# The first attention layer's opening, in a new order: single-ring loads, one row tile first, mask rows built between other steps

## The chip, the core and the metric

One core of a Trainium2 chip runs the whole program. The metric is device time in microseconds (us), from the median of several executions. One further execution was taken with the hardware profiler, and all durations below come from it. The engines are TensorE (PE, matmul), VectorE (DVE), ScalarE (ACT), GpSimd (POOL) and SyncE (SP, which only issues transfers). ACT and POOL can issue transfers too.

## The reference

Four layers, A B A B, over x of 2048 rows by 576, each with a layer norm in front and a residual behind. The change lies in the first A.

```python
def _A_ref(x, wqkv, wo):            # S = 2048, D = 576, H = 32 heads of Dh = 18
    W, dil = (8, 2)
    q, k, v = split(x @ wqkv)
    idx = pos[:, None] - arange(W) * dil      # each row looks at 8 rows, 2 apart
    mask = idx >= 0
    logits = where(mask, einsum(q, k[idx]) * Dh ** -0.5, -1e9)
    return einsum(softmax(logits), v[idx]) @ wo
x = x + _A_ref(_layernorm(x), A_wqkv, A_wo)
x = x + _B_ref(_layernorm(x), ...)           # gated MLP with a 2048 x 2048 row mix
x = x + _A_ref(_layernorm(x), A_wqkv, A_wo)
x = x + _B_ref(_layernorm(x), ...)
```

## The kernel before

x is cut into 16 row tiles of 128 rows. Each is normalised to bf16 (`ln_xn`, four buffers in rotation) and transposed into `xnT`, five chunks of 128 columns by all 2048 rows, from which everything else is projected.

Attention works on 19 query tiles (`NT`) of up to 112 rows, each with 16 rows of halo, in two half-steps of 16 heads, and takes dense 128 x 112 logits. Which keys a query may see is not masked afterwards. It is built into the product: Q and K of each head (18 rows) are extended to 32 rows in the tile `QK`, and the 14 added rows hold a fixed pattern whose product is strongly negative outside the window. The pattern repeats every 256 columns. `build_window_rows` (L115) makes one period in `win_rows`, stores it to DRAM (`win_period`, L166), `load_pat` (L168) reads it back four times into `win_pat`, and `fill_window_rows` (L181) copies it with DVE over one half of `QK`'s columns at a time (four copies of 4096 elements per partition, L190). Heads are then written over rows 0 to 17 of each group of 32.

The steps of the first layer's opening (L499 to L611), each a small function:

- `x_load`: a load of one to four row tiles. `load_wv`, `load_wqk`: the weights, 2 and 6 transfers.
- `S_`, `E_` on DVE: mean and variance of a tile (two L532 and one L533), plus epsilon (L536). `R_` on POOL: the power -1/2 (L539). `A_` on DVE: the normalised tile (L547).
- `T_pe`: five transposes on PE and a copy by ACT (L551, L556). `T_`: a transposing transfer on SP instead (L242).
- `VW(t, hh)` (L364): half of the values of query tile t, five matmuls, evacuated by ACT or DVE into `v_ext`. VW(t) needs rows 112t - 16 to 112t + 112. The last column of each head in `v_ext` holds ones (L517).
- `PG(d, qk, cc)` (L375): Q or K, columns 128d to 128d + 127, rows 512cc to 512cc + 511; five matmuls, evacuated into a staging tile `stg`. For the first 1024 rows, blocks d = 3 and 4 are staged in the space of `win2a` instead. When all parts of a block d for 1024 rows are there, it issues the head moves: one transfer of 72 KB per whole head from staging into `QK`, eight per block, dealt to the queues of POOL and SP in turn. For d = 4 the block holds Q and K side by side and only `PG(4, 0, cc)` exists.
- `L_mm(s)`, `EXP(s)`, `PV(s)` (L417, L431, L438): logits, exponential and value product of a half-step. `L_mm(0)` needs heads 0 to 15, `L_mm(1)` heads 16 to 31.

Behind the opening, the loop runs L_mm(s + 1), EXP(s + 1), PV(s) and whatever a table assigns to s: the remaining PGs (cc = 3 needs row tiles 12 to 15), values, the output projection, the next layer norm. Six PGs with cc = 2 stand between `L_mm(0)` and `L_mm(1)`.

What sets the order: `manual_schedule` (L341) keeps every engine's instructions in program order, so the order of the calls is the order on each engine and each queue. A transfer's issue blocks the issuing queue until its semaphores allow it. Transfers of SP and ACT share eight completion semaphores in rotation, so the issue also waits for the earlier transfer on the same semaphore.

The order before, around the PGs:

```python
order = [(d, cc) for cc in (0, 1) for d in (0, 1, 2)] + [(d, cc) for d in (3, 4) for cc in (0, 1)]
...
                if k_ == 3:
                    R_(8, 4)
                    A_(8, 9, 10, 11)
                    T_(8, 9, 10, 11)
                    S_(12, 13, 14, 15)
                    E_(12, 4)
                if k_ == 5:
                    self.fill_window_rows(QK, 1)
                    R_(12, 4)
                    A_(12, 13, 14, 15)
            T_(12, 13, 14, 15)
```

Of the kernel before, what the change touches and what calls it, by code (L numbers as in the profile page):

```python
# [10 lines left out]
ALU = mybir.AluOpType  # L11
AX = mybir.AxisListType
f32 = mybir.dt.float32
bf16 = mybir.dt.bfloat16
# [4 lines left out]
P = 128  # L19
D = 576  # L20
# [6 lines left out]
PADL = HALO  # L27
# [35 lines left out]
class K:  # L63
# [51 lines left out]
    def build_window_rows(self, c, eng):  # L115
# [31 lines left out]
        nc.vector.tensor_scalar(out=n[:], in0=n[:], scalar1=15, scalar2=None, op0=ALU.bitwise_and)  # L147
        nc.vector.tensor_scalar(out=g[:], in0=n[:], scalar1=1, scalar2=None, op0=ALU.logical_shift_right)
        nc.vector.tensor_tensor(out=g[:], in0=g[:], in1=n[:], op=ALU.bitwise_xor)
        for i in range(4):  # L150
            nc.vector.tensor_scalar(out=bits[:, i, :], in0=g[:], scalar1=i, scalar2=1,
                                    op0=ALU.logical_shift_right, op1=ALU.bitwise_and)
        nc.vector.tensor_scalar(out=bits[:, 4, :], in0=n[:], scalar1=1, scalar2=None, op0=ALU.bitwise_and)
        nc.vector.tensor_scalar(out=vf[:], in0=bits[:], scalar1=-2.0, scalar2=1.0, op0=ALU.mult, op1=ALU.add)
        nc.vector.tensor_scalar_mul(out=R[:, :, 0:8, :], in0=R[:, :, 0:8, :], scalar1=vf[:, 4, 1:2])
        nc.vector.tensor_tensor(out=uu[:], in0=vf[:, 0:4, 0:2], in1=vf[:, 0:4, 1:3], op=ALU.add)
        nc.vector.tensor_scalar_mul(out=R[:, 0, 8:12, :], in0=vf[:, 0:4, 1:2].to_broadcast([P, 4, 16]), scalar1=half)
        nc.vector.tensor_scalar_mul(out=R[:, 1, 8:12, 0:2], in0=uu[:, :, 0:1].to_broadcast([P, 4, 2]), scalar1=0.5)
        nc.vector.tensor_scalar_mul(out=R[:, 1, 8:12, 2:16], in0=uu[:, :, 1:2].to_broadcast([P, 4, 14]), scalar1=0.5)
        one = self.dram.tile([2, MR, 256], bf16, name="win_period")  # L160
        nc.gpsimd.memset(self.pat[:], 0.0)
        nc.gpsimd.memset(self.patpad[:], 0.0)
        for j in range(4):
            nc.gpsimd.affine_select(out=self.patpad[:], in_=self.patpad[:], compare_op=ALU.not_equal, fill=1.0,
                                    base=-32 * j - 31, pattern=[[0, PADL]], channel_multiplier=1)
        self.dma(one[:].rearrange("a r (p f) -> p (a r) f", f=16), R[0:16].rearrange("p a r f -> p (a r) f"), eng=eng)  # L166
# [4 lines left out]
        self.load_pat = load  # L171

    def make_ident(self):
        nc = self.nc
        for xb in self.xn_bufs:
            nc.gpsimd.memset(xb[:, D:640], 0.0)
        nc.gpsimd.memset(self.ident[:], 0.0)
        nc.gpsimd.affine_select(out=self.ident[:], in_=self.ident[:], compare_op=ALU.not_equal, fill=1.0,
                                base=0, pattern=[[-1, P]], channel_multiplier=1)
# [133 lines left out]
    def layer_A(self, li):  # L313
# [183 lines left out]


        if li == 0:  # L499
# [9 lines left out]
            x_load(x0[:, 0:2, :], 0, 2, nc.sync)  # L509
            x_load(x0[:, 2:4, :], 2, 2, nc.sync)  # L510
            self.load_wv(nc.scalar)
            x_load(x1[:, 0:4, :], 4, 4, nc.sync)
            self.load_wqk(nc.sync)
            self.zero_right()
            exp_table()
            self.build_window_rows(sb, nc.scalar)
            nc.scalar.copy(out=v_ext[:, :, :, DH:DH + 1], in_=self.ones[:, None, None, :].to_broadcast([P, NT, H, 1]))  # L517
            self.make_ident()
            setup_bufs(nc.gpsimd)
            x_load(spare, 8, 4, nc.sync)  # L520
            self.load_pat(nc.sync)
            warm = self.PT_tile([P, 512], f32, "warm")
            for _ in range(28):
                nc.tensor.matmul(warm[:, 0:P], lhsT=self.ident[:], rhs=self.ident[:], start=True, stop=True)
# [36 lines left out]
            S_(0, 1)  # L561
            E_(0, 2)
            R_(0, 2)
            S_(2)
            A_(0, 1)
            T_pe(0)
            T_pe(1)
            VW(0, 0, False)
            VW(0, 1, False)
            S_(3)  # L570
            E_(2, 2)
            R_(2, 2)
            VW(1, 0, False)
            VW(1, 1, False)
            S_(4)
# [3 lines left out]
            S_(5)  # L579
# [9 lines left out]
            R_(6, 2)  # L589
            A_(6, 7)  # L590
            T_(6, 7)
            x_load(sb.tile([P, 4, D], bf16, name="x_in3", tag="x_in", bufs=2)[:], 12, 4, nc.sync)
            self.fill_window_rows(QK, 0)
            S_(8, 9, 10, 11)
            E_(8, 4)
            order = [(d, cc) for cc in (0, 1) for d in (0, 1, 2)] + [(d, cc) for d in (3, 4) for cc in (0, 1)]
            for k_, (d, cc) in enumerate(order):
                for qk in ((1, 0) if d < 4 else (0,)):
                    PG(d, qk, cc, False, (nc.gpsimd, nc.sync) if d in (0, 4) else (nc.gpsimd, nc.gpsimd, nc.sync))
                if k_ == 3:  # L600
                    R_(8, 4)
                    A_(8, 9, 10, 11)
                    T_(8, 9, 10, 11)
                    S_(12, 13, 14, 15)
                    E_(12, 4)
                if k_ == 5:
                    self.fill_window_rows(QK, 1)
                    R_(12, 4)
                    A_(12, 13, 14, 15)
            T_(12, 13, 14, 15)  # L610
            nvw0, nvw = 3, 8  # L611
# [14 lines left out]
        q2 = (nc.gpsimd, nc.sync, nc.gpsimd)  # L626
# [395 lines left out]
```

The softmax here doesn't subtract the row's maximum and nothing guards it: scores larger than these inputs give would overflow.

## Time and profile before

| | us |
|---|---|
| median of 4 runs | 1202.51 (1200.61 to 1203.09) |
| the profiled execution, its own time | 1204.71 |
| its span, first to last instruction | 1202.9 |
| PE busy in the span | 1175.9 (98%) |
| DVE, ACT, POOL busy | 545.4, 377.9, 274.4 |
| first warm-up matmul; first VW; first PG | 5.71; 12.22; 18.48 |
| end of the last opening PG (d = 4, cc = 1) | 38.06 |

In the profile's rows, a line is: start, duration, engine, line of the code, operation, written tile <- read tiles, shape, count, and in brackets the engine's idle time before it and what ended that. SPq, ACTq are issues of transfers by those queues. A row of waits is: who <- for whom: us in total, times, longest. A row of windows is: the stretch, its length, then busy time and number of instructions of PE, PE's weight loads, DVE, ACT and POOL, then the granted PE clock (1.00 is full), the share of the transfer engines in use, and GB/s. A wait for several semaphores is put down to the one that the profile saw last.

### The profile page before, as it was taken

What the parts mean: (1) busy time and instruction counts of PE and PEld (TensorE: products, weight loads), DVE (VectorE), ACT (ScalarE), POOL (GpSimd) and SP (SyncE); (2) the same over time, 40 slices, a digit from 0 to 9 for tenths busy, and PEclk for the clock granted to TensorE, in tenths of its full rate; (3) what the DMA queues carried; (4) which work ended last, traced back from release to release, by engine and by line L of the source; (5) the groups of instructions that cost most, each with busy time, mean ns of one, the idle gap of its engine ahead of it and who ended that gap; (6) DMA issues with size and microseconds to landing.
All of it is one profiled execution on the core that took longest, in us unless ns stands there. A gap on an engine that the chain in (4) does not pass through costs nothing.

```text
span 1202.9 us, 20636 instructions
## 1 busy us (share of the span) xinstructions
PE 1175.9 (98%) x8438; PEld 620.6 (52%) x8536; DVE 545.4 (45%) x1199; ACT 377.9 (31%) x599; POOL 274.4 (23%) x381
## 2 busy tenths in 40 slices
PE   7899999999999999999999999999999999999998
PEld 4456644444444444447755765444444444444677
DVE  7577776432332332335454776763233323222321
ACT  4477777401111101101146786770110110111000
POOL 3558874100000000001135677640000000000000
PEclk9999999999999999999999999999999999999999
DMA  6789897000000000049646998900000000000432
GB/s 172 143 172 220 187 165 154 22 1 12 11 11 12 1 11 11 1 136 266 179 91 123 181 230 197 235 1 22 12 5 7 11 11 11 11 1 19 131 105 72
DMA packets 178185, 101.21 MB, mean 84 GB/s; under 512 B 135003, under 2 KB 159435, under 8 KB 178090
## 3 DMA queue, kind: packets, MB, share of 16 engines
q1 hardware_dynamic: 164330, 77.64, 30.6%
q0 software_dynamic: 6480, 15.96, 5.3%
q10 hardware_dynamic: 7280, 6.28, 1.7%
q8 instruction: 67, 1.10, 0.4%
q14 instruction: 28, 0.23, 0.1%
HBM read 42.39 MB, written 16.53 MB: 49 GB/s over the span
## 4 chain that ended last, share of the span: by engine, by line
PE 94%; DMA 3%; issue 1%; ACT 1%; POOL 1%; DVE 0%; SPq 0%; ACTq 0%; POOLq 0%; DVEq 0%
PE pg L856 41%; PE pz L838 12%; PE po L910 12%; PE pz L760 11%; PE pp L391 4%; PE pv L368 4%; PE pw L480 3%; PE O_ps L446 3%; PE L_ps L426 2%; PE pzs L760 1%; DMA oT<-o_t 1%; ACT P_sb L435 1%; POOL QK L77 1%; DMA wqk_sb<-in_A_wqkv_dram 1%; DMA QK<-win2a 0%
## 5 line engine op out<-in xcount | busy, mean ns | idle before, releaser
L856 PE MATMUL pg<-Wq,Z 128*128 128x512 bf16 x2256 | 500.3, 379 | 2.5
L856 PEld LDWEIGHTS <-Z 128*128 128x128 bf16 x2304 | 225.3, 98 | 272.0
L860 DVE TENSOR_TENSOR g_tmp<-pg,ln_xn 128x512 f32<-128x512 f32 x144 | 99.6, 692 | 429.1 <-PE pg L856 429.1
L850 ACT ACTIVATE z1T<-pz 128x1024 bf16<-128x1024 f32 x72 | 73.7, 1024 | 513.8 <-PE pz L838 513.6
L77 POOL DMA_DIRECT2D wout<-in_B_w_out_dram x4 | 4.2, 1062 | 604.6 <-PE pg L856 604.6
L435 ACT ACTIVATE P_sb<-L_ps 128x896 bf16<-128x896 f32 (+1 forms) x152 | 126.7, 887 | 48.7 <-PE L_ps L426 48.2
L910 PE MATMUL po<-wout,Z 128*128 128x288 bf16 x1152 | 141.4, 286 | 0.0
L838 PE MATMUL pz<-xnT,w 128*128 128x512 bf16 (+1 forms) x630 | 134.4, 380 | 1.6 <-issue 1.6
L910 PEld LDWEIGHTS <-Z 128*128 128x128 bf16 x1152 | 112.7, 98 | 28.8
L760 PEld LDWEIGHTS <-xnT 128*128 128x128 bf16 (+1 forms) x800 | 66.3, 97 | 80.9 <-issue 23.7
L760 PE MATMUL pz<-win2a,xnT 128*128 128x512 bf16 x366 | 103.5, 380 | 0.8
L861 DVE TENSOR_TENSOR Z<-g_tmp,z1T 128x512 bf16<-128x512 f32 x144 | 99.7, 692 | 9.7
L838 PEld LDWEIGHTS <-w 128*128 128x128 bf16 (+1 forms) x640 | 51.1, 97 | 80.0 <-issue 27.1
L391 PE MATMUL pp<-xnT,wqk_sb 128*128 128x512 bf16 x340 | 82.4, 385 | 4.6 <-DMA xnT<-ln_xn 3.5
L774 ACT ACTIVATE zp<-pz 128x1024 bf16<-128x1024 f32 x64 | 65.5, 1024 | 36.7 <-PE pz L760 33.9
L235 POOL TENSOR_SCALAR ln_xn<-x_new,ln_mv,ln_rstd 128x576 bf16<-128x576 f32 x32 | 73.4, 2294 | 2.8
L920 DVE TENSOR_TENSOR x_new<-po,xo 128x288 f32<-128x288 f32 (+1 forms) x64 | 28.8, 455 | 88.0 <-PE po L910 83.6
L760 PE MATMUL pz<-win2b,xnT 128*128 128x512 bf16 (+1 forms) x256 | 65.8, 380 | 0.0
L77 POOL DMA_DIRECT2D QK<-stg x81 | 51.7, 642 | 53.7 <-DVE stg L360 33.1
L776 DVE CUSTOM_DVE_ANT_0 Z<-zp 128x1536 bf16<-128x1536 bf16 x32 | 56.5, 1766 | 15.8 <-ACT zp L774 15.8
L368 PE MATMUL pv<-wv_sb,xnT 128*128 128x288 bf16 (+1 forms) x380 | 57.3, 291 | 2.8 <-DMA wqk_sb<-in_A_wqkv_dram 2.3
L391 PEld LDWEIGHTS <-wqk_sb 128*128 128x128 bf16 x360 | 33.5, 98 | 40.8 <-issue 5.3
(111 smaller groups left out, 885.6 us busy)
## 6 DMA issues: line engine op xcount, KB each, us to landing
xres<-x_new SPq DMA_DIRECT2D x48, 288.0 KB
xo<-xres SPq DMA_DIRECT2D x48, 288.0 KB
wout<-in_B_w_out_dram POOLq DMA_DIRECT2D x4, 1296.0 KB, 7.9
w<-in_B_w_in_dram SPq DMA_DIRECT2D x16, 256.0 KB
QK<-stg POOLq DMA_DIRECT2D x53, 72.0 KB, 4.4
QK<-stg SPq DMA_DIRECT2D x41, 72.0 KB
xo<-in_A_x_dram SPq DMA_DIRECT2D x16, 144.0 KB
win2a<-in_B_w_in_dram POOLq DMA_DIRECT2D x6, 288.0 KB, 5.2
```

Source lines behind the costliest of these rows:

```text
L77: return eng.dma_start(out=out, in_=in_)
L235: e.tensor_scalar(out=xn[:nrows, 0:D], in0=x_t[:nrows, :], scalar1=mv[:nrows, 0:1], scalar2=rstd[:nrows, 0:1], op0=ALU.subtract, op1=ALU.mult)
L368: nc.tensor.matmul(pv[:nk, 0:288], lhsT=self.xnT[:, c, QT * t:QT * t + nk], rhs=wv_sb[:, c, hh * 288:(hh + 1) * 288], start=(c == 0), stop ...
L391: nc.tensor.matmul(pp[:, :], lhsT=w, rhs=self.xnT[:, c, PADL + cc * 512:PADL + (cc + 1) * 512], start=(c == 0), stop=(c == 4))
L435: nc.scalar.activation(out=P_bufs[(2 * s + jp) % 4][:nk, :, :, 0:nq], in_=Lv[:nk, :, :, 0:nq], func=ACT.Exp, scale=scale)
L760: nc.tensor.matmul(pzvs[ci][:, sub * 512:sub * 512 + w], lhsT=self.xnT[r0:r1, c, PADL + i * P:PADL + (i + 1) * P], rhs=win2(c)[r0:r1, c0 + ...
L838: nc.tensor.matmul(pz1s[q // 2][:, q % 2, :], lhsT=w1[r0:r1, c, sub * P:(sub + 1) * P], rhs=self.xnT[r0:r1, c, PADL + q * 512:PADL + (q + ...
L850: nc.scalar.activation(out=z1T[:, q2 * 512:(q2 + 2) * 512], in_=pz1s[q2 // 2][:, :, :].rearrange("p a b -> p (a b)"), func=ACT.Gelu_apprx_ ...
L856: nc.tensor.matmul(pg[:, :], lhsT=Z[:, jj, i, sub * P:(sub + 1) * P], rhs=Wq[q][:, i, :], start=(i == 0), stop=(i == NS - 1))
L860: nc.vector.tensor_tensor(out=tmp[:], in0=pg[:, :], in1=bsp[:, qs], op=ALU.add)
L861: nc.vector.tensor_tensor(out=uT(jj)[:, sub, qs], in0=tmp[:], in1=z1Ts[jj, sub][:, qs], op=ALU.mult)
L910: nc.tensor.matmul(acc[hh], lhsT=uT(j // 2)[:, j % 2, i * P:(i + 1) * P], rhs=wouts[j // NJH][:, j % NJH, hh * 288:(hh + 1) * 288], start= ...
```

## The change

Only layer 0's opening changes, and `build_window_rows` is cut into pieces that are called later.

- Loads: tile 0 alone on SP and tile 1 alone on ACT, then tiles 2 and 3, wv, tiles 4 to 7, wqk, tiles 8 to 11, all on SP. wv was on ACT.
- `make_ident` comes before the rows on POOL; the warm-up has 46 matmuls instead of 28.
- Mask rows: the first eight DVE operations (`part0`) come before the statistics, POOL's pads and the buffer zeroing after `R_(1, 1)`, the last six DVE operations and the store to DRAM (`part1`) after `R_(2, 2)`. ACT's copy of ones into `v_ext` comes before the store.
- Tiles 0 and 1 are normalised each by itself; T_pe(0) is followed by VW(0), T_pe(1) by VW(1).
- The load of tiles 12 to 15 (x_in3) is issued before T_(4, 5). `load_pat` comes after T_(6, 7) instead of ahead of T_(4, 5). Tiles 8 to 11 are normalised and transposed before the PGs start, and `fill_window_rows(QK, 0)` comes behind that.
- The PGs run d = 0 to 3 with cc = 0, then VW(3), then d = 0 to 3 with cc = 1, then d = 4. The second fill comes after tiles 12 to 15 are normalised, instead of before.
- The queues of the moves are dealt in the pattern POOL, SP, POOL for d = 1, 2 and 3.

```diff
-            x_load(x0[:, 0:2, :], 0, 2, nc.sync)
+            x_load(x0[:, 0:1, :], 0, 1, nc.sync)
+            x_load(x0[:, 1:2, :], 1, 1, nc.scalar)
             x_load(x0[:, 2:4, :], 2, 2, nc.sync)
-            self.load_wv(nc.scalar)
+            self.load_wv(nc.sync)
             x_load(x1[:, 0:4, :], 4, 4, nc.sync)
             self.load_wqk(nc.sync)
+            x_load(spare, 8, 4, nc.sync)
+            exp_table()
             self.zero_right()
-            exp_table()
-            self.build_window_rows(sb, nc.scalar)
+            self.make_ident()
+            warm = self.PT_tile([P, 512], f32, "warm")
+            for _ in range(46):
+                nc.tensor.matmul(warm[:, 0:P], lhsT=self.ident[:], rhs=self.ident[:], start=True, stop=True)
+            rows = self.build_window_rows(sb)
             nc.scalar.copy(out=v_ext[:, :, :, DH:DH + 1], in_=self.ones[:, None, None, :].to_broadcast([P, NT, H, 1]))
-            self.make_ident()
-            setup_bufs(nc.gpsimd)
-            x_load(spare, 8, 4, nc.sync)
-            self.load_pat(nc.sync)
-            warm = self.PT_tile([P, 512], f32, "warm")
-            for _ in range(28):
-                nc.tensor.matmul(warm[:, 0:P], lhsT=self.ident[:], rhs=self.ident[:], start=True, stop=True)
+            rows[0]()
...
-            S_(0, 1)
-            E_(0, 2)
-            R_(0, 2)
-            S_(2)
-            A_(0, 1)
+            S_(0)
+            E_(0, 1)
+            R_(0, 1)
+            S_(1)
+            E_(1, 1)
+            R_(1, 1)
+            rows[1]()
+            setup_bufs(nc.gpsimd)
+            A_(0)
             T_pe(0)
-            T_pe(1)
             VW(0, 0, False)
             VW(0, 1, False)
-            S_(3)
+            A_(1)
+            T_pe(1)
+            VW(1, 0, False)
+            VW(1, 1, False)
+            S_(2, 3)
             E_(2, 2)
             R_(2, 2)
-            VW(1, 0, False)
-            VW(1, 1, False)
-            S_(4)
+            rows[2](nc.scalar)
             A_(2, 3)
             T_pe(2)
             T_pe(3)
-            S_(5)
+            x_load(sb.tile([P, 4, D], bf16, name="x_in3", tag="x_in", bufs=2)[:], 12, 4, nc.sync)
+            S_(4, 5)
...
+            S_(8)
             A_(6, 7)
             T_(6, 7)
-            x_load(sb.tile([P, 4, D], bf16, name="x_in3", tag="x_in", bufs=2)[:], 12, 4, nc.sync)
+            self.load_pat(nc.sync)
+            S_(9, 10, 11)
+            E_(8, 4)
+            R_(8, 4)
+            S_(12)
+            A_(8, 9, 10, 11)
+            T_(8, 9, 10, 11)
             self.fill_window_rows(QK, 0)
-            S_(8, 9, 10, 11)
-            E_(8, 4)
-            order = [(d, cc) for cc in (0, 1) for d in (0, 1, 2)] + [(d, cc) for d in (3, 4) for cc in (0, 1)]
+            S_(13, 14, 15)
+            E_(12, 4)
+            order = [(d, 0) for d in range(4)] + [(d, 1) for d in range(4)] + [(4, 0), (4, 1)]
             for k_, (d, cc) in enumerate(order):
                 for qk in ((1, 0) if d < 4 else (0,)):
-                    PG(d, qk, cc, False, (nc.gpsimd, nc.sync) if d in (0, 4) else (nc.gpsimd, nc.gpsimd, nc.sync))
+                    PG(d, qk, cc, False, (nc.gpsimd, nc.sync) if d in (0, 4) else q2)
                 if k_ == 3:
-                    R_(8, 4)
-                    A_(8, 9, 10, 11)
-                    T_(8, 9, 10, 11)
-                    S_(12, 13, 14, 15)
-                    E_(12, 4)
-                if k_ == 5:
-                    self.fill_window_rows(QK, 1)
+                    VW(3, 0, False)
+                    VW(3, 1, False)
+                if k_ == 6:
                     R_(12, 4)
                     A_(12, 13, 14, 15)
+                    self.fill_window_rows(QK, 1)
             T_(12, 13, 14, 15)
-            nvw0, nvw = 3, 8
+            nvw0, nvw = 4, 8
```

In `build_window_rows`, the same operations stand in three inner functions, `part0` (the bit patterns), `pads` (memsets of `pat` and `patpad` and four selects, on POOL) and `part1(eng)` (the last six DVE operations and the store), returned as `rows[0]`, `rows[1]`, `rows[2]`; the memsets of `ln_xn`'s last columns move there from `make_ident`. `q2` is `(nc.gpsimd, nc.sync, nc.gpsimd)`.

## The prediction

> **What bounds the kernel now.** I read the page first. TensorE (PE) is busy 98% of the span and 94% of the chain of work that ended last, so only PE idle time, or time at half clock, can be won. In the page's slices it lies in the first two and nowhere else that this change touches. So I asked for PE's waits in the first 90 us.
>
> ```profile
> PE warm L524 <- POOL ident L178: 5.7, 1, 5.7
> PE pp L391 <- DMA xnT<-ln_xn: 3.5, 1, 3.5
> PE pv L368 <- DMA wqk_sb<-in_A_wqkv_dram: 2.3, 1, 2.3
> ```
>
> Three waits: 5.7 us until the warm-up matmuls, 2.3 us before the first value projection (VW, L368), and 3.5 us later, before the first Q/K projection (PG, L391) that needs row tiles 12 to 15. The second is ascribed to a DMA, which does not fit: wv had landed by 6.9 us. The timeline of ACT shows the true releaser.
>
> ```profile
> 8.43 0.34 ACTq L77 DMA_DIRECT2D win_period<-win_rows  x1
> 8.81 2.82 ACT L517 COPY v_ext<-ones 128x608 bf16<-128x608 bf16 x1 [5.45 <-DVE ln_xn L547]
> 11.16 1.59 ACT L556 COPY xnT<-pt 128x640 bf16<-128x640 bf16 x2
> ```
>
> The mask-row store on ACT's queue issues only at 8.43 (it waits for the semaphore of an earlier load, x tiles 4 to 7, which landed at 8.3); behind it in ACT's order stands the copy of ones into v_ext, and behind that the copies that PE waits for. The 3.5 us wait is read from the timelines of SP and POOL.
>
> ```profile
> 32.41 6.42 SPq L242 DMA_TRANSPOSE xnT<-ln_xn  x4
> 38.93 4.27 SPq L77 DMA_DIRECT2D QK<-stg  x5
> 43.30 6.26 SPq L77 DMA_DIRECT2D QK<-win2a  x7
> 49.67 5.21 SPq L242 DMA_TRANSPOSE xnT<-ln_xn  x4
> ```
>
> ```profile
> 39.73 2.18 POOL L539 TENSOR_TENSOR lnx_rstd<-lnx_rstd,neg_half 128x4 f32<-128x4 f32 x1
> 41.62 5.16 POOL L77 DMA_DIRECT2D QK<-win2a  x9
> ```
>
> SP's head moves stand behind the transposes of tiles 8 to 11, and the transposes of tiles 12 to 15 behind the moves. The last move lands at 51.4 (POOL's) and PE waits 0.16 us for it in L_mm(1): move chain and PE run level there. That is the likely new bound. Last, the granted clock (PEclk), in windows laid on its steps:
>
> ```profile
> 10.17:13.59 3.42, 1.37 (x12) 1.10 (x13) 3.28 (x12) 2.98 (x4) 1.05 (x2) 1.00 1.13 309
> 13.59:17.00 3.41, 3.40 (x21) 2.34 (x18) 2.06 (x7) 1.71 (x4) 0.69 (x1) 0.50 0.11 22
> 51.13:54.55 3.42, 1.55 (x33) 0.98 (x32) 1.41 (x3) 1.73 (x2) 0.00 (x0) 1.00 0.68 130
> 54.55:57.96 3.41, 1.36 (x3) 0.58 (x5) 0.00 (x0) 0.00 (x0) 0.00 (x0) 0.50 0.73 178
> 57.96:61.37 3.41, 3.41 (x39) 1.35 (x37) 1.41 (x3) 1.73 (x2) 0.00 (x0) 0.50 0.20 70
> ```
>
> A 3.41 us window in which PE was busy 1.37 or 1.55 us is followed by one at 0.50. What half clock costs after the late wait: two attention steps from the PG at 56.38 take until 62.35, 5.97 us; the next two (62.35 to 66.50) 4.15 us. So 1.82 us for 4.99 us at half clock, or 1.24 us for one window.
>
> **The change part by part, the start.** ident moves to the head of POOL's work: memset and select, about 0.5 us from 0.9, so warm-up starts at 1.5 instead of 5.7. 46 matmuls by the 0.107 us between two of the 28 end at 6.4. They cover nothing PE needs earlier. DVE does the zeroing and part0 of the rows until 3.6, as before. Tile 0's load is 144 KB at the ring's head; the first two tiles landed at 4.3, half of that I put at 3.3 to 3.8. Then on DVE, by rows: S_ of one tile 1.05, E_ 0.17, S_(1) and E_(1) 1.2, A_(0) 0.4: ready at 6.5 (POOL's power, 0.7, lies under S_(1)). Five transposes, 0.5 cold; ACT's copy 0.7 with 0.15 before it: the first VW starts at 8.2, against 12.22. ACT is free, since the v_ext copy (2.8) now needs only ones and ends by 5.7. wv, now behind x on SP's ring: 1.25 MB in all, at the 340 to 390 GB/s of that stretch from 1.8, lands by 6.5: hidden by 1.7 us.
>
> Then a chain with its own gaps: VW(0) 1.23 (two of 0.61) and T_pe(1) to 9.75; ACT finishes the second evacuation (0.40), copies T_pe(1) 0.7: VW(1) at 10.85, a gap of 1.1. VW(1) and two transposes to 12.65. On ACT: the evacuation, then the row store (0.47 with its semaphore), then two copies: VW(2) at 13.95, a gap of 1.3; first PG at 15.2. POOL's pads and setup (2.75 us in its rows) end at 9.55, just where R_(2,2) wants to start. Before, full-rate PGs ran from 18.7: **gain 3.5 us**.
>
> [...] By the rows, half an idle window was enough. The two windows here would be busy 53 to 56%; the window before 98.92 was busy 1.86 of 3.41 (55%) and was followed by half clock too, though with smaller matmuls. So either nothing, or 1.2 to 1.5 us on the first PG. I take nothing, with even odds.
>
> **The middle.** Eighteen PGs by 1.08 and VW(3)'s 1.23, now inside, end 20.7 after the first PG: 35.9. Before, 38.06 and VW(3) behind it, 39.3: the same lead. Now what the moves wait for. Moves of block d=0 need both halves of d=0, the fifth place in the new order: 8.64 + 1.23 + 2.16 + 0.7 evacuation = 12.7, so 27.9; before they started at 27.9. They also need fill(0), now behind tiles 8 to 11 on DVE. From A_(2,3)'s end at 11.1 DVE has nine S_ at about 1.0, three E_ at 0.17, A_ of eight tiles at 0.36 and 0.4 of waiting: 23.8; then 0.3 + 4 copies at 1.15: 28.7. On SP: the x_in3 load (0.6, at 11.2), T(4..7) to 20.1, the four pattern loads 1.65, T(8..11) at 1.3 each to 27.6. So all head moves start at **28.7**, not earlier than before, although PE is 3.4 us ahead. That is where I expect gain to be held up.
>
> POOL has 24 of the 40 moves before and after. From 28.7: d=0, 2.64 as in its row; d=1 5 and d=2 6 at 0.60: 38.0; R_(12,4) 1.05 from its row at 30.86. DVE's A_(12..15) 1.45, then fill(1) from 40.6 to 45.2, beside POOL's moves of d=3 and d=4. The trace shows what that costs: within fill(1) before, POOL's two issues took 1130 and 1290 ns where nine others took 590 to 685, one POOL instruction per 1.22 us copy. Five issues at 0.60 become 1.15 for four of them: +2.2; before, the same fill cost 2.3 on the same queue, so this is no saving. POOL ends at 46.4 (before 46.78).
>
> [...] Landing: 3.4 us after the issue where the queue was unhurried (39.71 to 43.08), 4.6 at the end (46.78 to 51.35). I take 3.9: last landing **50.3**, bounds 49.8 and 51.0.
>
> PE: 35.9 + eight VW 4.9 = 40.8; L_mm(0) needs heads 0 to 15, whose last two moves are the first two of d=2 on POOL (issued by 35.6, landed by 39.5): no wait. Six PGs at 1.09, plus 0.3 because DVE evacuates them only after fill(1): PE reaches the end of L_mm(1) at 48.3 and waits **2.0 us**. Then 0.4 + 0.55, and the PG on tiles 12 to 15 starts at 51.3. SP, no longer behind transposes, does its 16 moves by 42.2, T(12..15) at 1.3 to 47.4, landed 1.4 later at 48.8: the 3.5 us wait goes. If the lanes were as slow as the T(8..11) row (1.6 each), 50: still in time.
>
> Sum, at the end of the second attention step after that PG: before 62.35; after 51.3 + 4.15 = 55.45, a gain of 6.9. The 2.0 us wait lies mostly in one window in 7 of 10 placings, hence one window at half clock: 1.24. **Gain 5.6 us.** Everything later is PE work in the same order, so I let it shift by as much. Span 1202.9 to 1197.3; with the 1.8 us around it (1204.71) 1199.1; against the median of the runs shown, 1202.51, **1196.9**.
>
> **Rivals.** (a) Moves land before PE needs them: POOL's issues overlap the fill less, and the wait and its half clock go. Gain 6.9 + 2.0 - 0 to 0.3: 8.6 to 8.9, so 1193.6 to 1193.9. For: SP's queue is freed of transposes and the last moves drain without backlog. Against: 28.7 and 24 issues. 0.18. (b) Half clock at both places, or a slow patch of transposes (one took 2.5 us in the trace) holding fill(0): 1.5 to 3 us lost, 1198.4 to 1200.1. 0.20. (c) Slower: POOL starved by fill(1). Each us that its d=3 and d=4 moves land later goes to PE at L_mm(1) in full. The gain is used up at 50.3 + 5.6 = 55.9, the point from which it decides; beyond 58.3 the kernel is slower by over 0.2%. [...] Nothing in the trace shows more than 1.29 us per issue. 0.07 for slower, 0.07 for within 0.2%. (d) The start gain is not real because x lands late on the one ring: then fill(0) sets the moves anyway and the loss at the end is under 1 us; inside the range.
>
> The likeliest has 0.48. A measurement tells about 0.2% (2.4 us): faster 0.86, same 0.07, slower 0.07. Range 1193.0 to 1200.2: from (a) through (b).
>
> **What would show it.** ACT's v_ext copy before 6 us; first VW near 8.2; first PG near 15.2; fill(0) ending and the first QK move at 28.7; a PE wait of about 2 us on a QK DMA at 50, in the place of the wait on xnT; POOL issues of about 1.2 us beside the second fill. I am wrong if that wait is absent, if L_mm(0) waits near 41, or if PE still waits for xnT.

## The result, and the profile after

| | before | after |
|---|---|---|
| median of the runs of one comparison, us | 1202.77 (57 runs, 1199.71 to 1205.6) | 1200.09 (38 runs, 1196.77 to 1205.03) |
| profiled execution, us | 1204.71 | 1202.5 |
| its span, us | 1202.9 | 1200.7 |
| second attention step after the first projection group on tiles 12 to 15 ends, us | 62.35 | 58.23 |

The ratio is 0.9983 (95% interval 0.9977 to 0.9990): faster by 0.17%, 2.0 us. I had forecast 1196.9, a gain of 5.6 us. The spans differ by 2.2 us. Executions of one kernel differ in how long the clock was halved (mean granted clock 0.993 to 0.999 over the 38 of the changed one): the profiled one of the changed kernel had a mean granted clock of 0.994 and is 2.4 us above the median, while 16 of the 38 runs had 0.997 and a mean time of 1199.8 us, so what follows is an account of an execution with more half clock than most. Below, the "lead" of a trace over that of before is the difference between the times at which the same exponential of the attention (ACT's P_sb) ends in the two.

TensorE's waits in the first 110 us of the changed kernel (total, times, longest, in us):

```profile
PE pw L487 <- DMA oT<-o_t: 3.1, 1, 3.1
PE L_ps L433 <- DMA QK<-win2a: 2.7, 4, 1.3
PE L_ps L433 <- ACT P_sb L442: 1.8, 4, 0.5
PE pv L375 <- ACT xnT L565: 1.5, 2, 0.8
PE warm L530 <- POOL ident L185: 1.5, 1, 1.5
```

The warm-up wait fell from 5.7 to 1.5 us, and the wait on xnT (3.5 us) is gone. In its place stand 2.7 us for the head moves in L_mm(1), which I had put at 2.0. The first line is one that I did not cost: the first layer's output projection (pw) waits for the transpose of o_t. It waited before as well, 1.9 us ending at 99.25; now 3.1 us ending at 96.35. The row of before:

```profile
PE pw L480 <- DMA oT<-o_t: 1.9, 1, 1.9
```

POOL's issues of the moves of d = 3 and 4 (fewest, median and most ns of one issue, then first and last start), after:

```profile
L77 POOL DMA_DIRECT2D QK<-win2a x9: 505/571/4885, 38.3 to 47.2; - x9
```

Eight of the nine are short; one took 4.885 us. It stands at 39.59 to 44.47, and the four copies of the second fill on VectorE at 39.74 to 44.37, each beginning before the last one's listed end. They touched in just the same way in the kernel before, and there two issues got through, one to a copy. These are the copies and POOL's issues beside them, first before, then after, then the changed kernel again at the third layer's fill:

```profile
37.26 4.62 DVE L190 COPY QK<-win_pat 128x4096 bf16<-128x4096 bf16 x4
L77 POOL DMA_DIRECT2D QK<-stg x2: 1130/1210/1290, 37.3 to 38.6; - x2
39.74 4.63 DVE L197 COPY QK<-win_pat 128x4096 bf16<-128x4096 bf16 x4
617.14 9.17 DVE L197 COPY QK<-win_pat 128x4096 bf16<-128x4096 bf16 x8
L77 POOL DMA_DIRECT2D QK<-stg x5: 1131/1138/1716, 620.2 to 625.3; - x5
```

What sets the long issue apart is when it began: 0.15 us ahead of the first copy. The short ones began under a copy and ended about 0.1 us after that copy's end, or, at 1.716, after the next one's.

The windows of the granted clock on its steps (columns as in the prediction: window, length, PE busy, PEld, DVE, ACT, POOL, PEclk, DMA share, GB/s):

```profile
47.49:50.90 3.41, 0.91 (x14) 0.42 (x10) 0.65 (x1) 0.18 (x1) 0.24 (x1) 1.00 1.10 180
50.90:54.32 3.42, 2.99 (x32) 1.31 (x37) 0.71 (x3) 1.59 (x2) 0.00 (x0) 0.50 0.37 120
54.32:57.73 3.41, 3.41 (x53) 1.52 (x45) 1.63 (x4) 1.73 (x2) 0.00 (x0) 0.50 0.14 27
91.86:95.28 3.42, 1.40 (x37) 0.93 (x32) 2.16 (x7) 2.02 (x3) 3.23 (x5) 1.00 0.97 154
95.28:98.69 3.41, 2.34 (x38) 1.45 (x39) 0.46 (x1) 0.34 (x1) 3.29 (x5) 0.50 1.15 271
98.69:102.10 3.41, 3.41 (x47) 2.06 (x44) 2.05 (x6) 1.71 (x3) 2.52 (x2) 0.50 0.97 268
```

Two windows at half clock follow L_mm(1)'s wait, where I had one, and two follow pw's wait, where the kernel before had one (98.92 to 102.33).

What delays oT is read from SP's timeline (start, length), after:

```profile
85.17 3.37 SPq L77 DMA_DIRECT2D QK<-stg  x4
88.66 1.23 SPq L249 DMA_TRANSPOSE xnT<-ln_xn  x1
89.99 0.53 SPq L77 DMA_DIRECT2D xo<-in_A_x_dram  x1
90.61 2.48 SPq L465 DMA_TRANSPOSE oT<-o_t  x1
93.19 1.22 SPq L249 DMA_TRANSPOSE xnT<-ln_xn  x1
```

The waiting pw needs the seventh transpose of o_t, the one issued at 90.61. Its o_t, counted as the seventh too, was written at 85.55. SP comes to it 5.06 us later, behind four moves, a row transpose (LN_T) and a load; the issue takes 2.48 us, and the transpose lands at 96.30, 10.75 us after its o_t. Before, the same transpose was issued 4.63 us after its o_t (94.29 after 89.67), behind the same kinds of transfer, and landed 9.54 us after it:

```profile
94.29 2.14 SPq L458 DMA_TRANSPOSE oT<-o_t  x1
```

TensorE comes to pw 7.7 us after that o_t in both, so the waits come out at 3.05 and 1.84 us, which fits the listed 3.1 and 1.9. Of the 1.2 us between them, 0.4 is SP's later issue and 0.8 the longer way from issue to landing. The traces list sixteen signals for the landing of each of these two transposes; after, fifteen had come by 94.74 and the last at 96.30, while before all sixteen came within 0.2 us (99.00 to 99.20). Without that straggler the wait would have been about 1.5 us (an estimate, 94.74 less 93.26). The first transpose of the stage, with an idle queue, is issued 0.06 us after its o_t and lands 2.5 us later, in both.

The lead is 4.11 us from 59 to 93 us without a change, 2.90 after pw's wait, and 1.92 at 102.7, after the half clock. There it stays until 610 us; another 0.3 us comes back by the end. So the gain was first 1.5 us too small at the prologue's end, and then 2.2 of the 4.1 us that there were went at one place 35 us later: 1.2 in the longer wait, 1.0 in the longer half clock.

### The profile page after: what moved, and what is told of

It is laid out like the page before. It is cut to its first block, busy times and chain, and to the rows that moved or that the text cites. A ratio compares the mean times of both kernels' runs of the same rounds, so it can differ in the third digit from the quotient of the medians.

```text
span 1200.7 us, 20675 instructions
## 1 busy us (share of the span) xinstructions
PE 1177.6 (98%) x8456; PEld 622.0 (52%) x8554; DVE 545.0 (45%) x1200; ACT 377.9 (31%) x599; POOL 276.7 (23%) x382
## 4 chain that ended last, share of the span: by engine, by line
PE 95%; issue 1%; DVE 1%; DMA 1%; ACT 1%; POOL 1%; POOLq 0%; DVEq 0%
PE pg L874 41%; PE pz L856 12%; PE po L928 12%; PE pz L778 11%; PE pp L398 6%; PE pw L487 3%; PE pv L375 3%; PE O_ps L453 3%; PE L_ps L433 2%; PE pzs L778 1%; ACT P_sb L442 1%; DMA oT<-o_t 0%; POOL QK L77 0%; DMA QK<-win2a 0%; DVE ln_st L541 0%
## 5 line engine op out<-in xcount | busy, mean ns | idle before, releaser
L487 PE MATMUL pw<-wo_sb,oT 128*128 128x288 bf16 x320 | 49.8, 291 | 4.0 <-DMA oT<-o_t 3.1
```

Of the source, the lines that this page charges most:

```text
L487: nc.tensor.matmul(pw[:, 0:288], lhsT=oT[:, c, r0:r0 + P], rhs=wo_sb[:, c, hh * 288:(hh + 1) * 288], start=(c == 0), stop=(c == 4))
```

## The experiments

All times are medians, and the ratio is to the kernel before as it was timed beside that run. That median lay between 1202.74 and 1204.81 us, so the ratios can be compared from row to row and the medians only roughly. The changed kernel itself stands at 0.9983 (0.9977 to 0.9990).

| run | median, us | ratio (95%) |
|---|---|---|
| e1: second fill late | 1198.51 | 0.9959 (0.9943 to 0.9976) |
| e2: new start, old middle | 1205.99 | 1.0019 (1.0010 to 1.0029) |
| e3: old start, new middle | 1205.91 | 1.0015 (1.0003 to 1.0027) |
| e4: dummy matmuls in the wait | 1202.03 | 0.9995 (0.9980 to 1.0010) |
| e5: projection a step later | 1199.67 | 0.9966 (0.9952 to 0.9979) |
| e6: LN_T a step later | 1199.22 | 0.9960 (0.9948 to 0.9973) |
| e7: win2a loaded earlier | 1200.19 | 0.9972 (0.9958 to 0.9986) |
| e8: e1 and e5 | 1197.35 | 0.9951 (0.9935 to 0.9966) |
| e9: before, projection later | 1203.32 | 1.0000 (0.9989 to 1.0012) |
| e10: second fill spread | 1197.87 | 0.9952 (0.9936 to 0.9968) |
| e11: e8, LN_T later too | 1195.63 | 0.9941 (0.9925 to 0.9958) |
| e12: e10, projection and LN_T later | 1193.49 | 0.9911 (0.9895 to 0.9927) |

**e1, the second fill out of POOL's way.**

```diff
                     A_(12, 13, 14, 15)
-                    self.fill_window_rows(QK, 1)
...
         for d, qk, cc in pre:
             PG(d, qk, cc, True, q2)
+        if li == 0:
+            self.fill_window_rows(QK, 1)
```

> The changed kernel with one edit: the second fill of the mask rows stands behind the six cc = 2 projections instead of behind A_(12..15). Theory A (POOL's moves are locked out by that fill, one issue of 4.88 us in the changed kernel): POOL's last issue ends near 43.4 instead of 47.7, the last move lands near 47.2 instead of 51.2, L_mm(1) waits under 0.4 us, no half clock follows; the second attention step after the opening ends near 53.4 instead of 58.2, so 4 to 5 us less than the changed kernel. Rival B (the transfers themselves set the pace, the issue only queues for them): the last landing stays within 1 us of 51.2 and the time within 1 us.

No issue is long any more, and 0.24% (2.9 us) is gained on the changed kernel (the intervals just clear each other); I had expected 4 to 5 us. L_mm(1) still waits 1.6 us, one half-clock window follows instead of two, and the lead at 57 us is 5.82 us instead of 4.11, although this trace reached its first projection group 1.1 us later (half clock at the start). So without the long issue 1.7 us more arrive, in this pair of traces. The last move landed at 50.70, within the 1 us of 51.2 that rival B named, but the time did move. The rest of the wait belongs to POOL's last issue, which stood 1.60 us behind a transfer:

```profile
44.41 0.51 POOL L77 DMA_DIRECT2D QK<-win2a  x1 [0.24 <-DMA QK<-stg]
46.52 0.51 POOL L77 DMA_DIRECT2D QK<-win2a  x1 [1.60 <-DMA QK<-win2a]
```

pw waits 2.9 us for oT here, and the lead falls from 5.73 to 3.70.

**e2 and e3, the two halves alone.** e2 is the kernel before with the new order up to T_pe(3) (with `load_pat` ahead of T_(4, 5)); e3 is the changed kernel with the old order up to there.

> The kernel before with the new start alone (loads, ident, warm-up, tile 0 alone, mask rows in pieces, up to the transposes of tile 3); from tile 4 on the old order. Theory A (before, the moves of d = 0 started 9.4 us after the first PG, set by PE, so an earlier PG brings earlier moves): first PG near 14.6 instead of 18.5, first move near 24, about 3 us less than before. Rival C (the start gain is lost wherever it is put, since T(8..11), POOL's powers and both fills fix the moves): first move not before 27 and under 1 us less than before.

> The changed kernel with the old start (first PG near 18.5). Theory A (moves wait for the fifth place in the new order, 12.7 us after the first PG, or for the first fill at 28.5): first move near 31.2, everything behind 2.7 us later than in the changed kernel, so about the time of before (1202 to 1203). Rival C (the start is without effect on the end of the opening): within 0.7 us of the changed kernel.

```profile
PE pp L398 <- DMA xnT<-ln_xn: 7.2, 2, 4.1
PE pw L487 <- DMA oT<-o_t: 3.4, 1, 3.4
```

These are e2's waits: the first projection group starts at 14.08, and TensorE then waits 4.1 us up to 24.8 for the row transposes of tiles 4 to 7, and 3.1 us up to 57.6. The first move starts at 29.88. Each half alone is slower than the kernel before, by 0.2%, where neither expectation had a slower time; only together do they gain. But the halves don't come apart cleanly. The new start stores the mask rows later (11.7 us instead of 8.4), and in the old middle `load_pat`, which reads them back, stands on SP ahead of those transposes: it issues at 16.28 instead of 14.62, and the transposes start behind it. So e2 does not show what the earlier start is worth by itself. In e3 the new middle waits 3.8 us in L_mm(1), its POOL issue again takes 4.88 us, and half clock follows.

**e4, the clock kept up.** 46 matmuls on the identity, of no use for the result, ahead of L_mm(1).

```diff
             PG(d, qk, cc, True, q2)
+        if li == 0:
+            warm = self.PT_tile([P, 512], f32, "warm")
+            for _ in range(46):
+                nc.tensor.matmul(warm[:, 0:P], lhsT=self.ident[:], rhs=self.ident[:], start=True, stop=True)
```

> The changed kernel with 46 extra warm-up matmuls (2.6 us at full clock) ahead of L_mm(1), where PE waits for the moves anyway. They change nothing that is computed. Theory A (two windows at half clock behind that wait cost about 2.4 us): the wait shrinks by 2.6, L_mm(1) ends as before at 51.3, the clock stays at 1.00 and the second attention step ends near 56 instead of 58.2; 1.5 to 2.4 us less. Rival D (the later wait on oT gives such gains back): under 0.7 us less at the end although the step ends earlier.

The clock stayed at 1.00 until 95.06 and the lead at 57 us rose to 6.37, 2.3 us more than in the changed kernel. Not all of it arrived: pw waited twice, 1.7 us ending at 74.5 and 2.3 us ending at 95.2, the lead was 4.0 at 101 us, and 3.0 at the end. The medians show no gain at all: the time can't be told from that of the kernel before or of the changed one. SP reached the seventh transpose 5.44 us after its o_t. TensorE wrote that o_t 4.5 us earlier than before, and SP issued its transpose 3.7 us earlier: the queue at the projection follows a lead only in part.

**e5, the projection given slack.**

```diff
+            late = 1 if li == 0 and t < NT - 5 else 0
+            s += late
             at(s - 5, XO, i)
...
-                at(s + 4, LN_T, i)
+                at(s + 4 - late, LN_T, i)
```

> The changed kernel with one number altered: in the first attention layer the output projection of row tiles 0 to 11 (WO, its statistics, its store and the loads of its residual) stands one attention step later, so that the transpose of o_t through SP's queue has a step (some 2 us) more to land; the normalised row's own transpose keeps its step. Theory F (the gain is given back at the wait of pw on oT, and at the half clock that this wait brings): no wait of over 0.5 us on oT up to 100 us, the half-clock stretch at 95 us gone or halved, and the lead of about 4 us over the kernel before, which stands at 95 us, still there at 105 us: 1198 to 1199 us where the changed kernel has about 1200.5. Rival G (the stage after is bounded by something else: the landing of the last row transposes or of win2b): the wait on oT goes, another one takes its place before 110 us, and the time stays at 1200 to 1201 us.

```profile
PE pw L487 <- DMA oT<-o_t: 1.0, 1, 1.0
```

pw's wait is 1.0 us (I had expected none over 0.5) and no half clock follows; one half-clock window is left in the whole attention stage, at 52. The ratio is 0.17% below the changed kernel's, which is what theory F asked (the median of 1199.67 is above its 1198 to 1199), but the two intervals touch, so the time alone does not prove it. The lead at 102 us can't be read here, since the order of TensorE's work there is another; at the stage's last exponential, where the orders are level again, it can, and that table stands below.

**e9, the control: the same edit in the kernel before.**

> The kernel before (old prologue) with the output projection of row tiles 0 to 11 of the first attention layer one attention step later, nothing else: the control for the two runs that gave the changed prologue this step. If the loss at the projection's wait on oT belongs to the earlier TensorE (the new prologue meets a wait that the old one met less), the old prologue gains less from the extra step than the new one did: its wait of 1.9 us and half a clock window, at most 2 us, so 1201 to 1202.5 us, and the two prologues, both with the later projection, stand 3.5 to 4.5 us apart. If the later projection is simply a better order that has nothing to do with the change, the old prologue gains the same 2 us or more from it and the prologues stay 2 to 2.7 us apart.

Its trace has no wait on oT up to 112 us (one of 0.7 us ends at 135.58), and yet its time is that of the kernel before: I had expected up to 1.5 us from it. With the later projection the two prologues stand 0.34% apart (e5 against e9, 4.1 us by the ratios), without it 0.17%. The gap between those two is no larger than the noise of the ratios, so the traces have to decide. This is the lead at two places, at the ninth exponential (55 to 66 us) and at the stage's last (130 to 140 us), in us:

| trace | ninth | last |
|---|---|---|
| after | 4.12 | 1.92 |
| e7 (loads earlier) | 4.75 | 2.06 |
| e6 (LN_T later) | 4.85 | 3.68 |
| e1 (fill late) | 5.82 | 3.69 |
| e4 (dummy matmuls) | 6.07 | 3.97 |
| e10 (fill spread) | 9.99 | 5.71 |
| e5 (projection later) | 5.40 | 5.78 |
| e8 (fill late, projection later) | 8.64 | 9.64 |
| e11 (e8, LN_T later too) | 7.00 | 8.45 |
| e12 (fill spread, projection and LN_T later) | 9.65 | 10.71 |
| e9 (before, projection later) | -0.61 | 1.72 |

Every trace of the new prologue without the later projection loses 1.2 to 4.3 us between the two places; none with it loses any. At the stage's end e5 is 4.06 us ahead of e9, the whole lead of the new prologue, where the changed kernel is 1.92 ahead of the kernel before. So the later projection is not simply the better order; it is what lets the new prologue's lead through. The table also shows how far one trace can be trusted: after, e5, e6 and e7 have the same prologue, and their leads at the ninth are 4.1 to 5.4 us. And the old prologue does gain from losing its wait, 1.7 us at the stage's end. Most of that goes in one wait at the head of the next layer, ending at 162.89, behind which the lead is 0.43 us (1.47 at the end of the span):

```profile
PE pz L762 <- ACT zp L776: 1.1, 1, 1.1
```

Why that wait appears I did not find, and the trace of before is itself of an execution 2.2 us above its median.

**e6 and e7, why oT is late.** e6 issues LN_T one step later (`at(s + 4 + (1 if li == 0 and t < NT - 5 else 0), LN_T, i)`); e7 issues the six loads of win2a at steps 5, 7, 9, 11, 1, 3 instead of 5, 7, ... 15.

> The changed kernel with one number altered: in the first attention layer the transposes of the normalised rows for the next layer (LN_T of row tiles 0 to 11) are issued one attention step later, so that the transpose of o_t does not stand behind one of them on SP (88.66 to 89.89 us, just ahead of the late one at 90.61). Nothing else moves. Theory F1 (SP's order is what makes oT late: a transpose of 1.23 us and its packets ahead of it): oT issued within 0.3 us of its o_t, the wait of 3.1 us falls below 1 us, and the time falls by 1.5 to 2 us to about 1198.7 us. Theory F2 (the transfer itself is slow beside win2a's load and the moves on POOL's queue, whatever stands ahead on SP): oT lands no more than 1 us sooner, the wait stays above 2 us, the time within 0.7 us of the changed kernel's.

> The changed kernel with the six loads of win2a issued on POOL at attention steps 1, 3 (the two pieces that no staged block uses) and 5 to 11 instead of 5 to 15, so that none of them is under way at 86 to 97 us beside the late transpose of o_t. Theory F2 (the load's packets slow the transpose): the wait on oT falls from 3.1 us to 1.5 us or less and the time by 1 us or more, to about 1199.3 us. Theory F1 (SP's order): the wait stays above 2.5 us and the time within 0.7 us of the changed kernel's. If an earlier oT wait opens near 70 us, where the loads then run beside other transposes, that too speaks for F2.

The 0.3 us in e6's expectation came from a misreading of mine, which took the transpose at 90.61 for that of the o_t at 89.91. By the count, the seventh transpose in e6 is issued 3.18 us after its o_t instead of 5.06, and lands 8.15 us after it instead of 10.75. The pw that waited 3.1 us for it now waits 0.49, up to 93.66 (put down to VectorE, but the transpose landed at 93.61). Smaller waits stand at other pw's: 0.77 us up to 74.78, 0.26 up to 98.41 and 1.15 up to 108.01. 0.23% is gained on the changed kernel, and the intervals do not overlap. e7's wait did not go:

```profile
PE pw L487 <- DMA oT<-o_t: 5.4, 3, 2.7
```

2.75 us ending at 95.88 and 2.31 us ending at 102.66. POOL's queue held the last load until 86.69, so it was not as early as planned, but it had landed at 89.97, ahead of the issue of the late transpose at 91.03. That issue came 5.61 us after its o_t, and the landing 10.41. So the wait does not need the loads (F2 falls as the main cause); it needs SP's lateness (F1), and LN_T is 1.9 us of that. The loads may still add to it: from issue to landing took 4.80 us here, without a straggler, and 5.69 in the changed kernel. But e4 has no straggler either, with the loads where they were. e7's time is 0.11% below the changed kernel's, more than I had expected under F1, but the intervals overlap.

**e8, both losses at once.**

> The fill of QK's second window rows put behind the six early projection groups (as in the run with the late fill), and the output projection one attention step later as well: both places where the trace shows the forecast gain going. If the two losses are separate, the sum holds: 1.7 to 2 us from the fill and 1.5 to 2 us from the projection's wait on the changed kernel's 1200.5, that is 1196.5 to 1197.5 us, near the forecast of 1196.9. If the oT wait is set by a queue that is full (rival D: whatever comes earlier on TensorE waits more there), a wait on oT or on P_sb of 1 us or more returns before 100 us and the time stays at 1198 to 1198.6 us, no better than the late fill alone.

```profile
PE L_ps L433 <- ACT P_sb L442: 1.0, 3, 0.4
PE L_ps L433 <- DMA QK<-win2a: 0.7, 2, 0.4
```

No wait on oT is listed between 30 and 112 us, and no half clock before 690 us. The time is inside what I had expected and near the forecast. Whether the two losses add up the times can't tell: e8 is 0.32% below the changed kernel, where e1's and e5's gains make 0.41%, and e8's interval overlaps e1's.

**e10, what makes the issue so long.** The four copies stand apart, one ahead of each of the second to fifth early projection group; the new third argument picks one copy.

```diff
...
                     A_(12, 13, 14, 15)
-                    self.fill_window_rows(QK, 1)
...
-        for d, qk, cc in pre:
+        for k_, (d, qk, cc) in enumerate(pre):
+            if li == 0 and k_ in (1, 2, 3, 4):
+                self.fill_window_rows(QK, 1, k_ - 1)
             PG(d, qk, cc, True, q2)
```

> The changed kernel with the four copies of the second window rows spread: one ahead of each of the second to fifth early projection group, with an eviction of VectorE between them, in place of four back to back behind the normalisation of tiles 12 to 15. It asks what makes POOL's issue take 4.88 us. If the lock lasts as long as one copy and only stretches because the copies touch (no gap in which POOL can get in), each overlapped issue takes 1.1 to 1.8 us, none over 2, POOL's last move is issued near 46.5 us and most of the late fill's gain is kept: 1198.5 to 1199.3 us. If the copies cost POOL the same sum wherever they stand, the issues add up to the same delay (last issue at 47.7 us) and the time stays within 0.5 us of the changed kernel's 1200.5.

```profile
L77 POOL DMA_DIRECT2D QK<-win2a x9: 505/587/1467, 37.6 to 43.2; - x9
```

```profile
PE pw L489 <- DMA oT<-o_t: 6.1, 2, 3.5
PE pv L377 <- ACT xnT L567: 2.3, 3, 0.8
PE L_ps L435 <- ACT P_sb L444: 1.5, 4, 0.4
```

The one issue that met a copy took 1.47 us (41.74 to 43.20, the copy 41.89 to 43.11): it began 0.15 us ahead of the copy, as the long one did, and ended 0.1 us after it. The expectation had the hold-up stretch because the copies touch. That alone is not it, since issues of 1.13 us got in between touching copies before and in the third layer. What fits every trace here is narrower: the issue of 4.885 us is in all six that keep the second fill where the change put it (after, e3 to e7), each time begun 0.15 to 0.16 us ahead of the first of the touching copies, and it ends 0.1 us after the last; an issue begun under a copy never took over 1.73 us. No run moves that start by itself, so the cause stays open. The spread copies also begin at 41.9, when most issues are through. TensorE waits for no head move at all, which is rival (a) of the prediction, and the lead at 53 us is 10.29; the time is below the range I had given. TensorE then loses 2.8 us at pw's first wait and 1.8 more at its second with the half clock: 5.72 is left at 99 us. SP is 5.82 us behind at the seventh transpose here, where it was 4.63 behind in the kernel before: it has the same work in less time. With the greater leads of e4 and e10 pw waits longer in all, 4.0 and 6.1 us against 3.1.

**e11 and e12, what the runs point to.** e11 is e8 with LN_T at `s + 4` of the later `s`; e12 is e10 with the projection and LN_T both one step later.

> The run with the late fill and the later projection, with the transposes of the normalised rows for the next layer (LN_T of row tiles 0 to 11) one step later too, so that they keep their distance from the projection. In that run the oT transposes are issued up to 3.3 us after their o_t, with no wait on TensorE: the slack is used. If SP's order still costs something there, this gives up to 1 us: 1196 to 1196.8 us. If TensorE has no wait left that SP can cause, the time stays within 0.5 us of 1197.4.

> The changed kernel with all that the runs point to: the second fill's four copies spread over the early projection groups, the first layer's output projection and the transposes of its normalised rows one attention step later. With the copies spread, TensorE had no wait at the second attention step and led the kernel before by 10.3 us at 61 us, of which two waits on oT (6.1 us) and a half-clock window left 5.9. If those waits go here, as they went with the late fill, 7 to 9.5 us of the lead stay at the end: 1193.5 to 1195.7 us. If SP's queue can't keep up with so early a TensorE (rival D at its strongest), waits on oT of 3 us or more stay, and the time is that of the run with the late fill and both later steps, 1195.6 us, or worse.

```profile
PE warm L532 <- POOL ident L185: 1.5, 1, 1.5
PE L_ps L435 <- ACT P_sb L444: 1.3, 4, 0.4
PE pw L489 <- DMA oT<-o_t: 0.7, 1, 0.7
PE L_ps L435 <- DMA QK<-win2a: 0.5, 1, 0.5
```

These are e12's waits. e11 came out at 1195.63, a little under its range; its interval overlaps e8's. e12 is the fastest, 0.89% ahead of the kernel before (10.7 us by the ratio). It is also the plainest test of the loss at the projection: it is e10 with the projection and LN_T a step later and nothing else, its ratio is 0.41% below e10's, and the intervals are well apart. Its five runs lie within 2.9 us (1192.08 to 1194.99), each at a mean granted clock of 1.000, where the 38 of the changed kernel lie within 8.3 us.

## Why the prediction was wrong

**Right: the start.** ACT's v_ext copy ran at 2.58 to 5.39 (I had it done by 5.7), the first VW started at 8.20 (8.2), the first projection group at 14.55 (15.2). That the two gaps would cost no clock was my estimate, at even odds. It held in the profiled run (1.00 from 6.53 to 50.90), but not always: in e1 the window 7.85 to 11.26 was at half clock and the first group came at 15.67.

**Right: where it is held up.** The head moves start at 27.66 on POOL and 28.47 on SP (28.7), the transposes of tiles 12 to 15 end their issue at 47.66 (47.4), L_mm(0) waits for nothing, xnT is not waited for, and L_mm(1) waits for the moves.

**Mis-sized: the second fill's cost on POOL.** I took four issues of 1.15 us by the row of the fill before, +2.2 us. One issue stood through all four copies: 4.88 against 0.59, +4.3 us. POOL ended at 47.73 instead of 46.4, the last landing was 51.22 instead of 50.3, the wait 2.7 instead of 2.0. So rival (c)'s mechanism, a POOL starved by the fill, is what happened, though short of the size at which the gain would have been used up (51.22, against 55.9); the chances that I gave (c) were my estimate. The row that I took was no bound even in its own trace: "Nothing in the trace shows more than 1.29 us per issue" overlooks one of 1.72 us at the third layer's fill (at 622 us). My price was too low. The long issue ended 0.11 us after the last copy's end (0.10 after its one copy in e10); why it had to outlast all four no run here shows. The group on tiles 12 to 15 started at 51.92 instead of 51.3, 0.6 us late, and a second half-clock window where I had taken one made the two steps behind it 0.9 us longer. Together the lead was 4.1 us instead of 5.6. e1, without the long issue, leads by 5.8; but e5, with it and with one half-clock window, leads by 5.4, so one window of half clock more or less moves this term by 1.3 us, nearly the whole shortfall.

**Failed: "Everything later is PE work in the same order, so I let it shift by as much."** This step lost 2.2 us of 4.1, and 4.6 of 10.3 in e10. The projection waits on a transpose that SP issues in the order of its queue, some 5 us late, and that wait stood in the trace of before, 1.9 us ending at 99.25, just behind the 90 us whose waits the prediction read. I knew the window before 98.92 for its half clock and did not ask why TensorE was idle there. e12 against e10 shows that the loss is there and what removes it, e5 against e9 that the lead comes through once pw has a step of slack, e6 against e7 that SP's order makes oT late. In the changed kernel's own trace, 0.8 of the 1.2 us by which the wait grew came from a slower transfer, most of it the straggler.

The sum for these two traces: forecast 5.6, less 1.5 at the prologue's end, less 2.2 at the projection, plus 0.3 that comes back after 610 us, 2.2, which is the difference of the spans.

**Luck.** The measured 1200.09 us lies inside the stated range, 0.1 us from its end, and at the edge of rival (b). Neither is to the prediction's credit: the half clock at both places and the held-up fill(0) of rival (b) are not what this trace shows, and the loss at the projection was in no rival.

**Open.** Why an issue begun just ahead of the copies waits out all four; why some transposes take 2.1 to 2.5 us to issue and others 1.2; where the straggler comes from; why e9 waits at 162.89.

## What to carry to other kernels

A gain made early is not a gain at the end until it has passed every wait behind it: read the waits of the whole stage, and treat each one that exists already as a place where a lead is taken back. Queue order is part of the schedule, so a transpose on which the bottleneck engine waits should not stand behind one that nobody needs yet (LN_T was 1.9 us of its lateness, e6); how late it is shows only when the k-th transpose is set against the k-th tile that it reads. Where one engine's copies hold up another's issues, a price read at one place need not hold at the next: the same four copies cost two issues 0.5 to 0.7 us each before and one issue 4.3 us after. Moving the copies away from the issues is safer than pricing them.

## What the hardware showed

POOL's transfer issues beside VectorE copies of 1.22 us: 4.88 us when the issue began 0.15 us ahead of four copies that touch, 1.47 us when it began as far ahead of one that stands alone (e10), and up to 1.72 us, mostly 1.13, when it began under one of a row of touching copies (before, after), against 0.5 to 0.7 us undisturbed. Those that were held ended about 0.1 us after the end of a copy.

Half clock could last a second window. After a window at half clock in which PE was busy 2.02 (e1, at 93.18), 2.34 and 2.99 us (after) or 3.14 us (e7, at 50.18) of 3.41, the next was at half clock too; after 3.30 (e4, at 95.06) or 3.41 it was not. Yet 3.09 us of wide matmuls (e1, at 7.85) and 3.08 us of mostly small ones (before, at 98.92) were followed by full clock, so busy time alone does not decide. The way down is as blurred: windows with 1.99 and 2.02 us busy at the start of the changed kernel were followed by 1.00, while in e8 a window of 2.88 us of mostly small matmuls, at 687 us, was followed by half clock. The falls at 50.90 and 95.28 (after), 7.85, 52.22 and 93.18 (e1), 95.06 (e4) and 50.18 (e7) came behind windows in which PE was busy for 0.91 to 2.02 us of 3.41, so none of those windows was idle throughout, and none of the waits was longer than 3.1 us.

In the trace of before, the first sixteen transfers of SP and ACT signal on eight semaphores, each used twice. The store of the mask rows, issued at 8.43, shares one with the load of x tiles 4 to 7, whose last signal came at 8.32; the first pattern load, at 14.62, stood behind a wait of SP that ended 0.02 us after the store's last signal (14.55).
